# Rounding by ACT, preparation in gaps, and the last expert products between the first blocks of the closing layer

## The chip, the core and the metric

The kernel runs on one core of a Trainium2 chip. The core has a matrix engine (PE), a vector engine (DVE), an engine for functions of one operand (ACT), a general engine (POOL), and queues that issue DMA transfers (SP's and ACT's for plain ones, POOL's for gathers by index). Each engine takes its instructions in the order in which the program lists them and waits on semaphores for the others. The metric is the device time of one execution in microseconds (us); lower is better.

## The reference, cut to what matters

Three steps run in a row: attention with keys and values pooled by 8 (8 batches, 8 heads, 576 tokens), a mixture of experts on its 4608 rows of 512, and a last layer.

```python
# experts: every row goes to the two best of 8
h = np.maximum(x[mask] @ w1[e], 0.0)                  # 512 -> 1024
out[mask] += top2_w[mask, k, None] * (h @ w2[e])      # 1024 -> 512
# last layer
h = x @ w_in                                          # 512 -> 2048
g = h * np.cos(h)
return (g @ w_out).astype(np.float32)                 # 2048 -> 512
```

## The kernel before

Every product of two float32 matrices is made from float16 halves: a value is a high part plus a rest, and three matmuls (high by high, high by rest, rest by high) give one product.

**Experts.** Rows are scattered to slots of their expert in memory. An expert's slots come in three chunks (`CH`): 512, 512 and 192. A job is one expert and one chunk, and `JOBS` lists them. A job makes eight first products (`mm1`, 12 matmuls each, with a relu on ACT and a rest on DVE behind each) and, for every 128 slots, one last product (`mm2`, 24 matmuls of 512 columns); `mix` spreads the last products of a job between the first products of the next. In the chunks of 192 the last 64 slots of two experts share one product (`mm2_pair`). ACT scales a finished product and stores it in `yb`. The program is one list, `work`; `begin` gives each entry a nominal time from its matmul columns, and `at` hangs other steps behind the first entry at or after a nominal time. So the order is written out by hand on every queue.

**Preparation of a chunk for the last layer.** A chunk is four tiles of 128 rows, and there are nine. Its steps: `gather` (POOL fetches the two expert rows of each row by index), `comb1a` (ACT) and `comb1b` (DVE) add them with their gates and take maxima, `comb2a` and `comb2b` make a scale from the chunk's maximum (through a small transpose on PE), and for each of seven operands `sub` (DVE), `opa` (ACT, high part), `opb` (DVE, rest, and a transposing DMA on SP's queue) fill the tile `xt_tile(c, o)`. Chunk 0 is prepared by `prepare_first` during the experts, at nominal times; chunk c + 1 by `prepare` while chunk c runs.

**Last layer.** A chunk runs in four quarters (`q_`) of its 2048 hidden columns. A quarter makes seven products (`prod`, numbers 1, 2, 6, 7, 5, 3, 4; 12 matmuls of 256 columns each) from which sums give four blocks of h, a scheme with seven products in place of eight. Each block then goes through `act_a` (DVE adds and subtracts a large constant, which rounds, and subtracts the rounded from the block; ACT takes the Sin and the Square) and `act_b` (DVE multiplies, ACT and POOL split the result into halves). The product with w_out (`down`, 3 matmuls of 512 columns each, 16 for a quarter) is listed in `ds` and taken from it by `some(n)` between the products of the following quarter. Products 1, 6, 5 and 3 use one PSUM bank (`pb`), so that each of the last three waits until ACT has copied the one before (copies at L1282, L1294 and L1302). `step` takes the next entry of the preparation at fixed places. The halves of w_out are loaded by `load_wout` into the buffers that the last two experts' `w2` leave.

Of the kernel before, what the change touches and what calls it, by code (L numbers as in the profile page):

```python
# [22 lines left out]
CAP = 1216  # L23
# [11 lines left out]
def tile_attn_moe_ffn(ctx: ExitStack, tc: tile.TileContext, q, k, v, wgate, wnoise, noise,  # L35
# [745 lines left out]
    JOBS = [(e, c) for e in range(E) for c in ((0, 1, 2) if e % 2 == 0 else (2, 0, 1) if e < E - 1 else (0, 2, 1))]  # L781
# [35 lines left out]

    def mm2(j, t):
        e, c = JOBS[j]
# [4 lines left out]
        ps = psum("py", 2)  # L824
        i = 0
        for f in range(8):
            for a_, b_ in ((0, 0), (0, 1), (1, 0)):
                PE.matmul(ps[0:m], ht[:, a_, f, 128 * t:128 * t + m], w[:, b_, f, :], start=(i == 0), stop=(i == 23))  # L828
                i += 1
        yt = wp.tile([128, 512], F32, name="yt", bufs=2)  # L830
        A.activation(yt[0:m], ps[0:m], AF.Copy, scale=W["y", e][0:m])  # L831
        r0 = E * o + n * e + 128 * t
        A.dma_start(yb[r0:r0 + m, :], yt[0:m])

    def mm2_pair(e):
        ps = psum("py", 2)

        w = [W["w2", e + i].rearrange("p s (k f) -> p s k f", k=8) for i in range(2)]
        i = 0
        for f in range(8):  # L840
            for a_, b_ in ((0, 0), (0, 1), (1, 0)):
                for h in range(2):
                    PE.matmul(ps[64 * h:64 * h + 64], TAIL[e + h][:, a_, f, :], w[h][:, b_, f, :], start=(i == 0),  # L843
                              stop=(i == 23))
                i += 1
        yt = wp.tile([128, 512], F32, name="yt", bufs=2)
        for h in range(2):
            hs = slice(64 * h, 64 * h + 64)
            A.activation(yt[hs], ps[hs], AF.Copy, scale=W["y", e + h][hs])
        for h in range(2):  # L850
            r0 = E * 1024 + (CAP - 1024) * (e + h) + 128
            A.dma_start(yb[r0:r0 + 64, :], yt[64 * h:64 * h + 64])
# [259 lines left out]
    def prepare(c, room):  # L1112


        def many(*x):
            return lambda: [f(c, *a) for f, *a in x]

        return [many((gather, 0), (gather, 1)),
                many((gather, 2), (gather, 3), (comb1a, 0), (comb1a, 1)),
                many((comb1b, 0), (comb1b, 1), (comb1a, 2), (comb1a, 3)),  # L1120
                many((comb1b, 2), (comb1b, 3), (comb2a,)),
                many((comb2b,), (opa, 0), (opa, 1), (opa, 2, room)),
                many((opb, 0), (opb, 1), (opb, 2), (sub, 3)),
# [222 lines left out]
```

## Time and profile before

| | |
|---|---|
| median of three runs | 1885.58 us (1883.87 to 1886.46) |
| profiled execution | 1891.88 us, span of the program 1890.1 us |
| PE busy | 1745.7 us, 92% of the span |
| DVE busy | 1193.2 us, 63% |
| ACT busy | 838.9 us, 44% |
| POOL busy | 421.6 us, 22% |
| DMA, mean over the span | 129 GB/s |

Busy is the time in which an engine works on an instruction; matmuls are pipelined and their ends are modelled, so that two that follow each other overlap a little. A row of a timeline gives the start in the span, the length, the engine, the line of the kernel, the operation, what it writes and reads, how many like it are merged, and in brackets how long the engine stood idle before it and what ended that.

### The profile page before, as it was taken

What the parts mean: (1) busy time and instruction counts of PE and PEld (TensorE: products, weight loads), DVE (VectorE), ACT (ScalarE), POOL (GpSimd) and SP (SyncE); (2) the same over time, 40 slices, a digit from 0 to 9 for tenths busy, and PEclk for the clock granted to TensorE, in tenths of its full rate; (3) what the DMA queues carried; (4) which work ended last, traced back from release to release, by engine and by line L of the source; (5) the groups of instructions that cost most, each with busy time, mean ns of one, the idle gap of its engine ahead of it and who ended that gap; (6) DMA issues with size and microseconds to landing.
All of it is one profiled execution on the core that took longest, in us unless ns stands there. A gap on an engine that the chain in (4) does not pass through costs nothing.

```text
span 1890.1 us, 28449 instructions
## 1 busy us (share of the span) xinstructions
PE 1745.7 (92%) x11160; PEld 1028.8 (54%) x11160; DVE 1193.2 (63%) x2160; ACT 838.9 (44%) x1699; POOL 421.6 (22%) x457
## 2 busy tenths in 40 slices
PE   5977772899999999999999997999999999999999
PEld 3655551455444644464445544666666666666665
DVE  5784765453657375526774144877878777787864
ACT  4765651232333233323333233555555555555554
POOL 1225446000000000001110012244242334424222
PEclk8988876899999999999999998999999999999999
DMA  9968334457362846465644443124131212313100
GB/s 277 300 240 301 113 109 161 136 169 222 102 200 83 223 119 221 123 200 125 200 145 115 176 156 101 34 73 69 55 90 29 79 35 76 80 41 89 35 28 23
DMA packets 233209, 243.50 MB, mean 129 GB/s; under 512 B 154352, under 2 KB 167664, under 8 KB 232432
## 3 DMA queue, kind: packets, MB, share of 16 engines
q1 hardware_dynamic: 210544, 183.97, 33.9%
q0 software_dynamic: 11520, 37.76, 6.1%
q10 hardware_dynamic: 11008, 19.93, 3.0%
q8 instruction: 88, 1.44, 0.3%
q14 instruction: 49, 0.40, 0.1%
HBM read 127.06 MB, written 78.12 MB: 109 GB/s over the span
## 4 chain that ended last, share of the span: by engine, by line
PE 46%; DVE 19%; ACT 11%; issue 4%; DMA 2%; ACTq 0%; DVEq 0%; POOL 0%; POOLq 0%; SPq 0%
PE ph L803 20%; PE py L828 20%; DVE ty L1231 5%; ACT ty L1232 5%; DVE ty L1230 4%; ACT ty L1233 4%; PE ph L1253 3%; DVE ty L1241 2%; PE py L1223 2%; DMA yg<-yb,yidx 2%; DVE ht L1099 1%; DVE ht L1290 1%; DVE x2h L1099 1%; PE py L843 1%; DVE x L1047 1%
## 5 line engine op out<-in xcount | busy, mean ns | idle before, releaser
L803 PE MATMUL ph<-xt,w 128*128 128x512 f16 (+1 forms) x2304 | 410.4, 336 | 8.8 <-DMA xt<-xs 8.8
L1253 PE MATMUL ph<-w,ht 128*128 128x512 f16 x1728 | 413.5, 379 | 0.0
L828 PE MATMUL py<-w,ht 128*128 128x512 f16 x1728 | 384.4, 379 | 0.0
L803 PEld LDWEIGHTS <-w 128*128 128x128 f16 x2304 | 214.9, 98 | 195.2 <-issue 13.8
L1243 POOL TENSOR_TENSOR ht<-ty,ht 128x512 f16<-128x512 f32 x144 | 181.5, 1271 | 467.1 <-ACT ht L1242 390.5
L816 DVE SCALAR_TENSOR_TENSOR ht<-ph,ht 128x512 f16<-128x512 f32 (+2 forms) x192 | 110.0, 574 | 266.2 <-ACT ht L815 266.1
L828 PEld LDWEIGHTS <-ht 128*128 128x128 f16 x1728 | 168.7, 98 | 198.8 <-DVE ht L816 0.5
L1253 PEld LDWEIGHTS <-ht 128*128 128x128 f16 x1728 | 169.3, 98 | 152.1 <-issue 0.8
L1223 PEld LDWEIGHTS <-st 128*128 128x128 f16 x1872 | 184.0, 98 | 90.5 <-issue 42.7
L1232 ACT ACTIVATE ty<-ty,k 128x512 f32<-128x512 f32 x144 | 104.0, 722 | 261.9 <-DVE ty L1231 243.6
L815 ACT ACTIVATE ht<-ph 128x512 f16<-128x512 f32 (+2 forms) x192 | 96.3, 502 | 180.5 <-PE ph L803 154.5
L1223 PE MATMUL py<-xt,st 128*128 128x256 f16 x1040 | 142.4, 276 | 21.8 <-ACT ht L1302 10.8
L831 ACT ACTIVATE yt<-py,ysc 128x512 f32<-128x512 f32 x72 | 49.4, 686 | 228.2 <-PE py L828 223.4
L1241 DVE SCALAR_TENSOR_TENSOR ty<-ty,ht 128x512 f32<-128x512 f32 x108 | 74.8, 692 | 110.7 <-ACT ty L1233 108.9
L1223 PEld LDWEIGHTS <-w 128*128 128x128 f16 x1152 | 113.2, 98 | 36.9 <-issue 1.0
L1223 PE MATMUL py<-w,st 128*128 128x256 f16 x832 | 111.7, 272 | 9.4 <-ACT ht L1294 6.7
L1032 POOL DMA_INDIRECT yg<-yb,yidx x72 | 73.4, 1020 | 162.9 <-DMA yb<-yt 93.5
L1231 DVE TENSOR_TENSOR ty<-ht,ty 128x512 f32<-128x512 f32 x108 | 104.9, 972 | 3.7
L894 POOL TENSOR_TENSOR tm<-yg 128x512 f32<-128x512 f32 x32 | 33.8, 1055 | 302.6 <-DVE x L904 150.5
L1242 ACT ACTIVATE ht<-ty 128x512 f16<-128x512 f32 x144 | 90.1, 626 | 24.6 <-DVE ty L1241 24.4
L450 PE MATMUL xp<-vbd,et 128*64 128x144 f32 (+3 forms) x864 | 80.5, 326 | 17.7 <-DVE g_u L492 17.7
L1230 DVE TENSOR_SCALAR ty<-ht,k 128x512 f32<-128x512 f32 x108 | 91.1, 843 | 7.7
(249 smaller groups left out, 2141.6 us busy)
## 6 DMA issues: line engine op xcount, KB each, us to landing
yb<-yt ACTq DMA_DIRECT2D x72, 256.0 KB
st<-in_moe_w_dram SPq DMA_DIRECT2D x8, 2048.0 KB
yg<-in_moe_w_in_dram SPq DMA_DIRECT2D x32, 512.0 KB
yg<-in_moe_w_out_dram SPq DMA_DIRECT2D x32, 512.0 KB
yb<-zt SPq DMA_DIRECT2D x18, 768.0 KB
st<-in_moe_w_dram SPq DMA_DIRECT2D x8, 1536.0 KB
w<-in_k_dram SPq DMA_DIRECT2D x16, 512.0 KB
w<-in_v_dram SPq DMA_DIRECT2D x16, 512.0 KB
```

The costliest lines, as they stand in the source:

```text
L803: PE.matmul(ps[:, 0:n], w[:, a_, k_, 128 * f:128 * f + 128], xt[:, 4 * b_ + k_, 0:n], start=(i == 0), stop=(i == 11))
L815: A.activation(t[:, 0], p, AF.Relu)
L816: V.scalar_tensor_tensor(t[:, 1], p, 0.0, t[:, 0], op0=OP.max, op1=OP.subtract)
L828: PE.matmul(ps[0:m], ht[:, a_, f, 128 * t:128 * t + m], w[:, b_, f, :], start=(i == 0), stop=(i == 23))
L1223: PE.matmul(o, FW["in"][4 * a_ + 2 * sa + k_][:, f:f + 128], x[:, :, sb, k_, :], start=(start and h == 0 and k_ == 0 and j == 0), stop=(k_ ...
L1230: V.tensor_scalar(y, h, k4[:, 0:1], k4[:, 0:1], op0=OP.add, op1=OP.subtract)
L1231: V.tensor_sub(y, h, y)
L1232: A.activation(y, y, AF.Sin, scale=k4[:, 1:2])
L1241: V.scalar_tensor_tensor(y, y, CC, h, op0=OP.subtract, op1=OP.mult)
L1242: A.activation(g[:, 2 * b, :], y, AF.Copy)
L1243: PL.tensor_sub(g[:, 2 * b + 1, :], y, g[:, 2 * b, :])
L1253: PE.matmul(ps, g[:, 2 * b + a_, 256 * h + 128 * tt:256 * h + 128 * tt + 128], FW["out"][b_][:, k_, :], start=(q_ == 0 and b < 2 and h == ...
```

## The change

- `JOBS`: the last expert's chunks go in the order 0, 1, 2; before, 0, 2, 1.
- `mm2` and `mm2_pair` can be made in parts. The last `mm2` (of the last expert's chunk of 192) and the last `mm2_pair` leave `work` and become the first eight entries of `ds`, four parts each, in the PSUM banks `ph`. They are taken between the products of chunk 0's first quarter, and `load_wout` moves in there.
- `prepare_first`: nominal distances of 1.3 instead of 1.8, and the steps from 15 on (`own_first`) go into chunk 0's first quarter.
- `act_a` and `act_b` become five steps placed one by one. `act_r`: ACT adds the constant. `act_t`: one DVE operation subtracts the constant and the block. `act_s`: Sin and Square. `act_b`: DVE's product. `act_g`: the split by ACT and POOL. The copy at what was L1294 stands ahead of block 0's Sin and Square where it stood behind them.
- `prepare` returns steps under names of places in a quarter (A1, V1, V2, A2, V3, G1, G2) instead of one list; the gathers for a chunk come half a chunk earlier, from the third chunk on.

```diff
-    JOBS = [(e, c) for e in range(E) for c in ((0, 1, 2) if e % 2 == 0 else (2, 0, 1) if e < E - 1 else (0, 2, 1))]
+    JOBS = [(e, c) for e in range(E) for c in ((0, 1, 2) if e % 2 == 0 or e == E - 1 else (2, 0, 1))]
...
+    def parts(k_, fs, ps, done):
+        st = []
+        n = len(fs) // k_
+        def part(i):
+            def f():
+                if i == 0:
+                    st.append(ps())
+                for m in fs[n * i:n * i + n]:
+                    m(st[0])
+                if i == k_ - 1:
+                    done(st[0])
+            return f
+        return [part(i) for i in range(k_)]
...
+        if c == 1:
+            put_(0, "G1", (gather, 0), (gather, 1))
+            put_(0, "G2", (gather, 2), (gather, 3))
+            put_(1, "A1", (comb1a, 0), (comb1a, 1))
+            put_(1, "V2", (comb1b, 0), (comb1b, 1))
+            put_(1, "A2", (comb1a, 2), (comb1a, 3))
+            put_(1, "V3", (comb1b, 2), (comb1b, 3), (comb2a,))
+            put_(2, "A1", (comb2b,))
+        else:
+            put_(0, "A1", (comb1a, 0), (comb1a, 1), (comb1a, 2))
+            put_(0, "V2", (comb1b, 0))
+            put_(0, "A2", (comb1a, 3))
+            put_(0, "V3", (comb1b, 1))
+            put_(1, "V1", (comb1b, 2))
+            put_(1, "V2", (comb1b, 3), (comb2a,))
+            put_(1, "V3", (comb2b,))
+        put_(2, "A1", (opa, 0), (opa, 1), (opa, 2, room))
+        put_(2, "V1", (opb, 0))
+        put_(2, "V2", (opb, 1), (sub, 3))
+        put_(2, "A2", (opa, 3))
+        put_(2, "V3", (opb, 2), (sub, 4), (sub, 5))
+        put_(3, "A1", (opa, 4), (opa, 5, room))
+        put_(3, "V1", (opb, 3), (sub, 6))
+        put_(3, "V2", (opb, 4), (opb, 5))
+        put_(3, "A2", (opa, 6))
+        put_(3, "V3", (opb, 6))
+        if c + 1 < NCF:
+            for q_ in (2, 3):
+                st[q_, "G1"] = [lambda i=i: gather(c + 1, i) for i in (2 * q_ - 4, 2 * q_ - 3)]
+        return st
...
-    for j in range(NJ + 1):
+    for j in range(NJ):
...
-    sched[work.index((mm2_pair, E - 2))].append(load_wout[0])
...
+    own_first = []
...
-            at(begin[o] + 12 + 1.8 * (t - 3), f)
+            (own_first.append if t >= 15 else lambda f: at(begin[o] + 12 + 1.3 * (t - 3), f))(f)
...
-    def act_a(c, q_, b, h):
-
-        k4 = CB["k4", c]
+    def act_r(c, q_, b, h):
+
         y = wp.tile([128, 512], F32, name="ty", bufs=4)
-        V.tensor_scalar(y, h, k4[:, 0:1], k4[:, 0:1], op0=OP.add, op1=OP.subtract)
-        V.tensor_sub(y, h, y)
-        A.activation(y, y, AF.Sin, scale=k4[:, 1:2])
+        A.activation(y, h, AF.Identity, bias=CB["k4", c][:, 0:1])
+        UB[b] = (c, q_, h, y)
+
+    def act_t(b):
+
+        c, _, h, y = UB[b]
+        V.scalar_tensor_tensor(y, y, CB["k4", c][:, 0:1], h, op0=OP.subtract, op1=OP.subtract)
+
+    def act_s(b):
+
+        c, _, _, y = UB[b]
+        A.activation(y, y, AF.Sin, scale=CB["k4", c][:, 1:2])
         A.activation(y, y, AF.Square, scale=math.sqrt(2.0 * CC))
...
-    load_wout[1]()
-    ds, st = [], []
+
+    bank = lambda: psum("ph", 4)
+    ds = mm2_pair_parts(E - 2, 4, bank) + mm2_parts(NJ - 1, 0, 4, bank)
...
             prod(c, q_, 1, pb, True)
             A.activation(cw[:, 0], pb, AF.Copy)
-            act_b(2)
-            if q_ == 0 and c and st:
-                step()
-            if q_ == 0 and c + 1 < NCF or q_:
-                step()
+            if 2 in UB:
+                act_b(2)
+                act_g(2)
+            if c == 0 and q_ == 0:
+                for f in own_first:
+                    f()
+                some(1)
+            at_("A1")
+            at_("V1")
             some(2)
             prod(c, q_, 2, pa, True)
             V.tensor_add(cw[:, 0], pa, cw[:, 0])
-            act_a(c, q_, 0, cw[:, 0])
+            act_r(c, q_, 0, cw[:, 0])
+            act_t(0)
             some(2)
             prod(c, q_, 6, pb, False)
             A.activation(cw[:, 1], pb, AF.Copy)
+            act_s(0)
+            at_("V2")
+            if c == 0 and q_ == 0:
+                load_wout[0]()
             some(2)
             prod(c, q_, 7, pc, True)
+            if c == 0 and q_ == 0:
+                some(1)
+                load_wout[1]()
             act_b(0)
-            if len(st) > 1 or q_ < 3:
-                step()
+            act_g(0)
+            at_("G1")
+            at_("A2")
+            at_("V3")
             some(1)
             prod(c, q_, 5, pb, False)
             A.activation(cw[:, 2], pb, AF.Copy)
             V.tensor_add(cw[:, 2], pc, cw[:, 2])
-            act_a(c, q_, 3, cw[:, 2])
+            act_r(c, q_, 3, cw[:, 2])
+            act_t(3)
             some(2)
             prod(c, q_, 3, pb, False)
-            act_a(c, q_, 1, pb)
+            act_r(c, q_, 1, pb)
+            act_t(1)
+            act_s(3)
+            act_s(1)
             act_b(3)
+            act_g(3)
+            at_("G2")
             some(1)
             prod(c, q_, 4, pc, False)
             V.tensor_add(cw[:, 1], pc, cw[:, 1])
+            act_r(c, q_, 2, cw[:, 1])
             act_b(1)
-            act_a(c, q_, 2, cw[:, 1])
+            act_t(2)
+            act_g(1)
             some(16)
+            act_s(2)
```

## Rows read from the trace of the kernel before

**Rows 1.** The profile's page: busy time of each engine, and from its list of groups the Sin (line, engine, operation, tiles, shapes, count | busy us, mean ns | idle us before it and what ended it).

```profile
PE 1745.7 (92%) x11160; PEld 1028.8 (54%) x11160; DVE 1193.2 (63%) x2160; ACT 838.9 (44%) x1699; POOL 421.6 (22%) x457
...
L1232 ACT ACTIVATE ty<-ty,k 128x512 f32<-128x512 f32 x144 | 104.0, 722 | 261.9 <-DVE ty L1231 243.6
```

**Rows 2.** The table of stretches in the last layer: the stretch, its length, busy us (and instructions) of PE, PE's weight loads, DVE, ACT and POOL, granted clock of PE, share of the DMA engines, GB/s.

```profile
1306.16:1327.66 21.50, 19.85 (x133) 12.88 (x132) 13.52 (x17) 11.90 (x20) 13.81 (x14) 1.00 0.41 111
...
1817.26:1836.79 19.53, 19.53 (x134) 12.91 (x133) 12.20 (x16) 11.01 (x18) 4.76 (x5) 1.00 0.11 42
1190.00:1870.00 680.00, 661.43 (x4436) 433.64 (x4434) 508.96 (x730) 381.92 (x617) 227.68 (x190) 1.00 0.22 57
```

**Rows 3.** The waits of PE from 1190 us to the end: who waited for whom, us in total, times, longest.

```profile
PE py L1223 <- ACT ht L1294: 13.2, 23, 1.1
PE py L1223 <- ACT ht L1302: 4.8, 7, 1.3
```

**Rows 4.** The timeline of the quarter that begins at 1306.16, around PE's wait: the sum on DVE, the Sin, the copy, the product that waits.

```profile
1313.16 0.68 DVE L1290 TENSOR_TENSOR ht<-pt,ht 128x512 f32<-128x512 f32 x1
...
1315.32 0.72 ACT L1232 ACTIVATE ty<-ty,k 128x512 f32<-128x512 f32 x1 [3.25 <-DVE ty L1231]
...
1316.61 0.58 ACT L1294 ACTIVATE ht<-py 128x512 f32<-128x512 f32 x1
...
1317.24 1.47 PE L1223 MATMUL py<-xt,st 128*128 128x256 f16 x12 [1.14 <-ACT ht L1294]
```

**Rows 5.** Single lines of the kernel over the span: line, engine, operation, count, shortest/median/longest in ns, first and last start, shapes.

```profile
L1230 DVE TENSOR_SCALAR ty<-ht,k x108: 545/548/1408, 1142.9 to 1873.9; 128x512 f32<-128x512 f32 x108
L1230 DVE TENSOR_SCALAR ty<-py,k x36: 799/805/811, 1158.9 to 1870.3; 128x512 f32<-128x512 f32 x36
...
L1231 DVE TENSOR_TENSOR ty<-ht,ty x108: 691/693/1529, 1143.5 to 1875.4; 128x512 f32<-128x512 f32 x108
...
L1241 DVE SCALAR_TENSOR_TENSOR ty<-ty,ht x108: 682/692/694, 1145.6 to 1878.4; 128x512 f32<-128x512 f32 x108
...
L1243 POOL TENSOR_TENSOR ht<-ty,ht x144: 1152/1161/1612, 1153.5 to 1879.8; 128x512 f16<-128x512 f32 x144
```

**Rows 6.** The timeline of PE from the last experts into the last layer, and its last stretch. L803 is `mm1`, L828 `mm2`, L843 `mm2_pair`, L1223 `prod`, L1253 `down`.

```profile
1064.25 2.14 PE L803 MATMUL ph<-xt,w 128*128 128x192 f16 x24
...
1080.55 5.34 PE L828 MATMUL py<-w,ht 128*128 128x512 f16 x24
...
1086.82 0.40 PE L843 MATMUL py<-w,ty 128*64 128x512 f16 x1
...
1092.12 2.76 PE L803 MATMUL ph<-xt,w 128*128 128x512 f16 x12
1094.72 5.34 PE L828 MATMUL py<-w,ht 128*128 128x512 f16 x24
1099.90 10.52 PE L803 MATMUL ph<-xt,w 128*128 128x512 f16 x48
...
1118.57 20.88 PE L828 MATMUL py<-w,ht 128*128 128x512 f16 x96
1139.29 1.47 PE L1223 MATMUL py<-xt,w 128*128 128x256 f16 x12
...
1156.14 2.71 PE L1223 MATMUL py<-xt,st 128*128 128x256 f16 x12 [8.54 <-ACT ht L1302]
...
1162.18 1.47 PE L1223 MATMUL py<-xt,w 128*128 128x256 f16 x12 [0.78 <-DVE ht L1311]
...
1174.76 2.61 PE L1223 MATMUL py<-xt,st 128*128 128x256 f16 x12 [2.62 <-ACT ht L1294]
...
1186.18 1.47 PE L1223 MATMUL py<-xt,w 128*128 128x256 f16 x12
...
1871.96 14.41 PE L1253 MATMUL ph<-w,ht 128*128 128x512 f16 x66
```

**Rows 7.** The timeline of DVE, ACT and POOL in the same stretch: a gather (L1032), two combinations (L1047), a rest and the wait for its landing (L1099, L1095), the combination that waits for a gather (L1041) and the copy behind it (L1302).

```profile
1089.59 1.02 POOL L1032 DMA_INDIRECT yg<-yb,yidx  x1 [93.50 <-DMA yb<-yt]
...
1105.31 0.74 DVE L1047 SCALAR_TENSOR_TENSOR x<-yg,gates,x 128x512 f32<-128x512 f32 x1
...
1106.69 0.74 DVE L1047 SCALAR_TENSOR_TENSOR x<-yg,gates,x 128x512 f32<-128x512 f32 x1
...
1114.83 0.74 DVE L1099 SCALAR_TENSOR_TENSOR x2h<-x,xt4s,x2h 128x512 f16<-128x512 f32 x1
...
1118.47 0.72 ACT L1095 ACTIVATE x2h<-x,xt4s 128x512 f16<-128x512 f32 x1 [1.69 <-DMA xt<-x2h]
...
1152.17 0.72 ACT L1041 ACTIVATE x<-yg,gates 128x512 f32<-128x512 f32 x1 [5.18 <-DMA yg<-yb,yidx]
...
1155.52 0.58 ACT L1302 ACTIVATE ht<-py 128x512 f32<-128x512 f32 x1
```

**Rows 8.** The issue of w_out's second half on SP's queue (timeline), and two rows of the table of stretches (columns as in rows 2).

```profile
1139.49 0.32 SPq L1177 DMA_DIRECT2D w<-woutd  x1
...
1140.00:1144.00 4.00, 4.00 (x40) 3.59 (x38) 1.75 (x3) 0.78 (x2) 0.00 (x0) 1.00 0.94 324
...
1172.00:1176.00 4.00, 1.38 (x8) 0.92 (x7) 2.42 (x5) 2.47 (x4) 0.32 (x1) 0.86 0.00 0
```

**Rows 9.** The groups of ACT over the span: all loads of a table of functions.

```profile
L60 ACT ACT_TABLE_LOAD x1 | 1.3, 1283 | 0.7 <-PEq L1331 0.7
L730 ACT ACT_TABLE_LOAD x1 | 1.3, 1283 | 0.0
```

More of the change, by code (lines that the diff above doesn't have):

```diff
@@ L816, in mm1, with mm2_parts @@
             V.scalar_tensor_tensor(t[:, 1], p, 0.0, t[:, 0], op0=OP.max, op1=OP.subtract)
+    def parts(k_, fs, ps, done):
[11 more added lines that the diff above has]
+        return [part(i) for i in range(k_)]
     def mm2(j, t):
+        for f in mm2_parts(j, t, 1, lambda: psum("py", 2)):
+            f()
+    def mm2_parts(j, t, k_, bank):
         e, c = JOBS[j]
@@ L823, in mm2, with done, mm2_pair_parts @@
         ht = HT[j]
-        ps = psum("py", 2)
-        i = 0
+        fs = []
         for f in range(8):
             for a_, b_ in ((0, 0), (0, 1), (1, 0)):
[L828 to L833, printed above, removed]
+                fs.append(lambda ps, i=len(fs), f=f, a_=a_, b_=b_: PE.matmul(
+                    ps[0:m], ht[:, a_, f, 128 * t:128 * t + m], w[:, b_, f, :], start=(i == 0), stop=(i == 23)))
+        def done(ps):
+            yt = wp.tile([128, 512], F32, name="yt", bufs=2)
+            A.activation(yt[0:m], ps[0:m], AF.Copy, scale=W["y", e][0:m])
+            r0 = E * o + n * e + 128 * t
+            A.dma_start(yb[r0:r0 + m, :], yt[0:m])
+        return parts(k_, fs, bank, done)
     def mm2_pair(e):
-        ps = psum("py", 2)
+        for f in mm2_pair_parts(e, 1, lambda: psum("py", 2)):
+            f()
+    def mm2_pair_parts(e, k_, bank):
         w = [W["w2", e + i].rearrange("p s (k f) -> p s k f", k=8) for i in range(2)]
-        i = 0
+        fs = []
         for f in range(8):
@@ L842, in mm2_pair, with done @@
                 for h in range(2):
[L843 to L852, printed above, removed]
+                    fs.append(lambda ps, i=len(fs) // 2, f=f, a_=a_, b_=b_, h=h: PE.matmul(
+                        ps[64 * h:64 * h + 64], TAIL[e + h][:, a_, f, :], w[h][:, b_, f, :], start=(i == 0), stop=(i == 23)))
+        def done(ps):
+            yt = wp.tile([128, 512], F32, name="yt", bufs=2)
+            for h in range(2):
+                hs = slice(64 * h, 64 * h + 64)
+                A.activation(yt[hs], ps[hs], AF.Copy, scale=W["y", e + h][hs])
+            for h in range(2):
+                r0 = E * 1024 + (CAP - 1024) * (e + h) + 128
+                A.dma_start(yb[r0:r0 + 64, :], yt[64 * h:64 * h + 64])
+        return parts(k_, fs, bank, done)
     def y_rows():
@@ L1112, in prepare, with put_ @@
     def prepare(c, room):
[L1115 to L1123, printed above, removed]
-                many((sub, 4), (sub, 5), (opa, 3), (opa, 4), (opa, 5, room)),
-                many((opb, 3), (opb, 4), (opb, 5), (sub, 6)),
-                many((opa, 6), (opb, 6))]
+        if c >= NCF:
+            return {}
+        st = {}
+        def put_(q_, p_, *x):
+            st.setdefault((q_, p_), []).extend((lambda f=f, a=a: f(c, *a)) for f, *a in x)
+        if c == 1:
[28 more added lines that the diff above has]
+        return st
     load_x(0)
@@ L1268, in some, with at_ @@
         del ds[:n]
-    def step():
-        if st:
-            st.pop(0)()
     for c in range(NCF):
+        plan = prepare(c + 1, lambda: g[:, 14:16, :])
         for q_ in range(4):
-            if q_ == 0 and c + 1 < NCF:
-                st += prepare(c + 1, lambda: g[:, 14:16, :])
+            def at_(p_):
+                for f in plan.pop((q_, p_), []):
+                    f()
             g = GQ[c, q_] = wp.tile([128, 16, 512], F16, name="ht", bufs=2)
```

10 lines of the change are left out of this document (5 added, 5 removed).

## The prediction, made before the change was run

> **What bounds the kernel now.** I read the page first: the matrix engine (PE) is busy for 1745.7 of 1890.1 us [rows 1], so only its idle time can be won. The table of stretches then shows where the change can reach. From 1190 to 1870 us, the last layer, PE is busy for 661.43 of 680 us at full granted clock [rows 2]. A quarter of a chunk in which nothing waits (1817.26 to 1836.79) takes 19.53 us, all of it busy; the quarter at 1306.16 takes 21.50 us [rows 2]. The view of waits gives the cause: PE waits 13.2 us for the ACT copy at L1294 and 4.8 us for the one at L1302 [rows 3].
>
> The timeline of such a quarter shows why the copy is late [rows 4]. ACT takes its instructions in order. The copy of product 6 (L1294) stands behind the Sin and the Square of block 0, the Sin waits 3.25 us for DVE's two rounding operations, and DVE reaches the sum at L1290 late because of preparation work. PE then stands 1.14 us. Over the span the Sin stands 243.6 us idle behind DVE [rows 1].
>
> The second place is the passage from the experts to the last layer, 1080 to 1186 us. The PE timeline shows chunk 0's first quarter lasting from 1139.29 to 1162.18 and the second to 1186.18, with waits of 8.54 and 2.62 us [rows 6]. ACT's copy L1302 came late because the combination of the next chunk's rows stood ahead of it in the queue, 5.18 us waiting for a gather [rows 7]; that gather waits for the last expert's second chunk, which is the last thing that PE makes before the layer.
>
> **The rounding.** Each block loses one DVE instruction (548 ns from SBUF, 805 from PSUM) and has one of 693 ns (L1231) replaced by another two-input one; I price that by L1241, 692 [rows 5]. ACT gets one more per block, priced like the Sin with its per-partition operand, 722 ns [rows 1]. The bounds are 0.58 (the copy L1294, [rows 4]) and 0.72; both change nothing, since ACT is busy 11.90 of 21.50 us in a slow quarter [rows 2] and four more instructions make it 14.8 of 19.5.
>
> What decides is the order. After the change ACT does: add for block 0, copy of product 6, then Sin and Square. In the quarter shown, the sum starts at 1313.16 [rows 4]; with 0.69 for it and 0.72 for the add, ACT is free at 1314.6, the copy is done at 1315.2, and PE would come for it at 1316.1. It is 0.9 early instead of 1.14 late. What is late next? Product 3 needs the copy of product 5 with one pair of `down`s (1.30) as cover; copy and handoff take 0.8, so 0.5 is left. The first product of the next quarter needs the sum at L1311, which now stands behind the add, Sin and Square and the product of other blocks: 0.2 + 0.72 + 0.72 + 0.63 + 0.69 + 0.69 = 3.7 from the end of product 3, covered by a `down`, product 4 and six more `down`s, 5.8. Both covers hold.
>
> Sum: from 1186.18 to 1871.96 [rows 6] are 685.8 us for 34 quarters, less six `down`s left over (18 of the 66 matmuls of 14.41 us, 3.9). At 19.53 each that is 660.1 us. Of the 25.7 lost the two waits make 18.0 [rows 3], and their pipeline ends and other small delays the rest. I take back 23 and leave 0.08 a quarter.
>
> A rule speaks against this edit. The Trainium skill (ScalarE: Activation LUTs, section Rules for kernel authors) says that adds belong on VectorE, not ScalarE. By the instruction alone it would be right: 722 against 548 ns, 144 times, 25 us more engine time, and the sum would lose that if ACT were the bound. The trace doesn't bear it out here, since ACT stands 243.6 us waiting for DVE.
>
> **The passage.** The last expert's slots go in the order first, second, third chunk; the third's last product and the paired one leave the stretch before the layer and fill the first quarter. Lengths from [rows 6]: 12 matmuls of 512 columns 2.6 us, 12 of 192 columns 1.0, a last product of 24 5.2, the pair 5.3. The last `mm2` of the first chunk starts at 1080.55 now; seven first products of 2.6 instead of 1.0 stand before it, so 1091.8 then. From there the work alone is 5.2 + 2.6 + 8 x 1.0 + 4 x 5.2 = 36.6, the first quarter 19.53 - 10.5 (no `down`s yet) + 5.3 + 5.2 = 19.5, the second 19.53: it would end at 1167.4, 18.8 before today's 1186.18. I expect these stalls on it:
> - The PE transpose of the chunk's maximum is queued after the fifth first product of the last job, about 23.0 us after that `mm2`'s start. Its input comes after the rounding of the fourth product on DVE (22.9), two combinations at the pitch of 1.38 [rows 7], and 0.7 for maximum, copy and handoff: 26.4. So 3.4 us. Today's order, with 1.8 for 1.3 between the steps and longer products beside them, hides it.
> - Four operands of the layer's products are made inside the first quarter, on ACT, DVE and SP's queue. One goes from DVE to landed in 2.9 us (1115.57 to 1118.47, [rows 7]). Product 6 needs the sixth; by this chain it is there 11 us into the quarter, PE at 9.1: 1.8 us.
> - The copy of product 5 stands on ACT behind the eviction of the last expert's product (0.7) and the split of block 0 (0.6); they start 0.2 after that product, and product 5 covers 1.3 of this. With the copy's own 0.6 PE loses 0.9.
> - The quarter ends without `down`s, so of the 3.7 us above only 1.3 is covered: 2.4.
> - The second half of the layer's output weights (2048 KB) can be asked for only when the last expert part is done, 17.5 into the quarter. At 324 GB/s [rows 8] it takes 6.5 us, plus 3.2 for four gather transfers of 256 KB sharing the engines: landed at 24.4 to 27.6, and the first `down` comes at 25.9. I take 1.5, with 0 and 4 as bounds. SP's queue holds only later operands behind it, POOL's only the third chunk's gathers.
> - The clock. After 2.62 us of idle PE the granted clock was 0.86 over 1172 to 1176 [rows 8], between the levels of 2.4 and 1.2 GHz, and 12 matmuls took 2.61 instead of 1.47 us [rows 6]. For two stalls of that length I take 2.5, bounds 0 and 6.
>
> Together 12.5, so the passage gives 18.8 - 12.5 = 6.3, between 0 and 13. The gathers' own wait goes: the second chunk's rows are stored a whole job before. The new parts use the `ph` banks, free until the first `down`; the expert evictions move to ACT's idle time; the preparation's other steps are the same instructions at other places and cost nothing as long as DVE, lighter by some 2.4 us a quarter, keeps up.
>
> **The sum.** 23 + 6.3 = 29.3. The profiled execution took 1891.88 around its span of 1890.1 and would take 1862.6; it lies 6.3 above the median of the three runs, 1885.58, from which I take the same off: 1856.3, said as 1857. About 0.2% (4 us) is what this measurement can tell from no change.
>
> **Rivals.**
> - The wait moves (0.22). The new DVE operation of a block has two SBUF inputs like L1231, which went from 693 to 1529 ns [rows 5] where POOL's subtraction (1.16) ran. If sums or copies slip by that 0.8 behind a cover of 0.5, PE loses 0.2 to 0.5 us a quarter, 7 to 17 us: 1863 to 1874. Against it: DVE has less to do and the exposed block is the last of a quarter, with 3 us of cover.
> - The passage gives nothing (0.12): weights, gathers and clock take 6 to 12 more, the layer still gains its 23: 1862 to 1871.
> - Slower (0.09): ACT doesn't reach the copy of product 5 in time. With a Sin and Square of one block (1.35) ahead of it at that point, beyond the 0.5 of cover each us of lateness costs 34 us. It decides at 1.4 us of lateness, where the 29 is gone; at 2 us it is 1907. For it: 14.8 us of work in order in 19.5. Against it: nothing ahead of that copy waits for DVE's backlog any more.
> - The add needs another table of functions on ACT (0.02): two loads a block at 1283 ns [rows 9], 10.3 a quarter, ACT at 25 us a quarter: some 2060. Against it: the whole profile has two loads, though Relu, Copy, Square and Sin take turns. The Trainium skill (ScalarE: Activation LUTs, section Table sets: the hidden batching unit) has identity in every set as a cheap filler. By that no load comes; the trace agrees for Copy.
> - No change (0.03): DVE stays late from the preparation alone and the passage gives back the rest.
>
> **The numbers.** The forecast has 0.52, with a range of its own from 1848 to 1866 (25 and 12, or 18 and 2). The range reaches through the first two rivals and stops short of the others: 1847 to 1875, some 0.82. Faster 0.86, same 0.03, slower 0.11.
>
> **What would show it.** Right: in the stretch after the second quarter the waits of PE for the two copies sum to under 3 us, quarters of 19.5 to 19.7, DVE's share down and ACT's up by 12 to 15 points, no third table load. The first quarter starts near 1132 and the third near 1180, with stalls at the transpose, product 6 and the first `down`. Wrong: a quarter over 20 us in the steady part, a wait of PE on an ACT add, Sin or on L1311, or a start of the third quarter after 1186.

## The result and the profile after

The changed kernel takes 1854.05 us (median of six runs, 1850.7 to 1861.98), the kernel before, beside it, 1885.22 (1883.87 to 1892.08): a ratio of 0.9839 with a 95% interval of 0.9814 to 0.9865, so faster by 1.4 to 1.9%. The profiled execution took 1861.98 with a span of 1859.9, 29.9 below the 1891.88 of the one of before; the prediction's sum was 29.3.

The page of the changed kernel, busy time of each engine; before is [rows 1].

```profile
PE 1734.3 (93%) x11160; PEld 1025.2 (55%) x11160; DVE 1063.2 (57%) x2016; ACT 928.3 (50%) x1843; POOL 424.0 (23%) x457
```

DVE has lost 130 us and ACT gained 89.

The table of stretches of the changed kernel (columns as in [rows 2]): the whole steady part, the first quarter of chunk 2, and five short stretches of the passage, where the clock is of interest.

```profile
1200.00:1840.00 640.00, 639.93 (x4332) 423.51 (x4331) 374.98 (x574) 453.97 (x732) 221.18 (x184) 1.00 0.22 57
1297.80:1317.33 19.53, 19.53 (x134) 12.91 (x132) 10.01 (x15) 14.76 (x24) 4.46 (x4) 1.00 0.01 3
...
1116.00:1120.00 4.00, 1.85 (x9) 0.94 (x10) 3.60 (x15) 0.00 (x0) 0.00 (x0) 1.00 0.00 0
1120.00:1124.00 4.00, 4.00 (x24) 2.07 (x23) 0.05 (x1) 0.30 (x1) 0.00 (x0) 1.00 0.00 0
...
1152.00:1156.00 4.00, 2.21 (x21) 1.83 (x19) 2.51 (x5) 3.67 (x6) 2.99 (x4) 1.00 1.01 430
1156.00:1160.00 4.00, 3.20 (x16) 1.76 (x16) 2.30 (x3) 3.17 (x6) 3.47 (x4) 0.70 0.75 299
...
1160.00:1164.00 4.00, 4.00 (x25) 2.48 (x24) 1.39 (x2) 3.15 (x6) 3.38 (x4) 0.87 0.63 195
```

From 1200 to 1840 PE stands 0.07 us; the view of waits lists none on PE from 1190 to 1860, where before had 13.2 and 4.8 [rows 3]. The first quarter of chunk 2 takes 19.53 against 21.50 [rows 2]. In it, from the timeline of the changed kernel (L1355 the sum, L1360 the copy of product 6, L1294 the Sin):

```profile
1300.40 1.47 PE L1277 MATMUL pt<-xt,w 128*128 128x256 f16 x12
1301.97 0.69 DVE L1355 TENSOR_TENSOR ht<-pt,ht 128x512 f32<-128x512 f32 x1 [2.07 <-PE pt L1277]
...
1304.52 0.60 ACT L1360 ACTIVATE ht<-py 128x512 f32<-128x512 f32 x1 [1.04 <-PE py L1277]
1305.01 0.71 ACT L1294 ACTIVATE ty<-ty,k 128x512 f32<-128x512 f32 x1
```

DVE waits 2.07 us for PE and starts the sum 0.1 us after product 2, where before it started 2.8 us after it (mean of the first quarters of chunks 1 to 7, from the trace). ACT waits 1.04 for product 6 and copies it at once.

The timeline of PE in the passage of the changed kernel, the rows that wait and the ends of the stretch (L110 the transpose, L1277 `prod`, L1314 `down`); before is [rows 6].

```profile
1118.15 0.33 PE L110 MATMUL pt<-idf,mbc 128*128 128x128 f32 x1 [3.22 <-DVE mbc L104]
...
1131.65 1.47 PE L1277 MATMUL py<-xt,w 128*128 128x256 f16 x12
...
1142.43 1.48 PE L1277 MATMUL py<-xt,st 128*128 128x256 f16 x12 [1.07 <-DMA xt<-x2h]
...
1151.42 1.47 PE L1277 MATMUL py<-xt,st 128*128 128x256 f16 x12 [1.00 <-DMA yb<-yt]
...
1156.43 1.61 PE L1277 MATMUL py<-xt,w 128*128 128x256 f16 x12 [2.23 <-DVE ht L1392]
...
1158.83 2.29 PE L1314 MATMUL ph<-w,ht 128*128 128x512 f16 x5 [0.36 <-DMA w<-woutd]
...
1171.96 1.47 PE L1277 MATMUL py<-xt,st 128*128 128x256 f16 x12 [1.04 <-ACT ht L1377]
...
1175.20 0.38 PE L1277 MATMUL py<-xt,w 128*128 128x256 f16 x2 [1.11 <-DVE ht L1378]
...
1180.39 1.47 PE L1277 MATMUL py<-xt,w 128*128 128x256 f16 x12
...
1841.75 14.41 PE L1314 MATMUL ph<-w,ht 128*128 128x512 f16 x66
```

The third quarter starts at 1180.39 instead of 1186.18: the passage gave 5.8. From there to the last 66 matmuls it is 661.4 instead of 685.8 us: the steady part gave 24.4. Both are near the forecast. What each came from is another matter.

### The profile page after: what moved, and what is told of

It reads as the page before. It is cut to its first block, busy times and chain, and to the rows that moved or that the text cites. A ratio compares the mean times of both kernels' runs of the same rounds, so it can differ in the third digit from the quotient of the medians.

```text
span 1859.9 us, 28283 instructions
## 1 busy us (share of the span) xinstructions
PE 1734.3 (93%) x11160; PEld 1025.2 (55%) x11160; DVE 1063.2 (57%) x2016; ACT 928.3 (50%) x1843; POOL 424.0 (23%) x457
## 4 chain that ended last, share of the span: by engine, by line
PE 77%; ACT 2%; DVE 1%; DMA 1%; issue 0%; another core or an unknown queue 0%; ACTq 0%; SPq 0%
PE ph L803 21%; PE ph L1314 19%; PE py L847 19%; PE py L1277 14%; PE pt L1277 2%; PE py L869 1%; DMA xt<-x2h 1%; DMA xt<-xs 0%; DVE x L1076 0%; DVE ty L1289 0%; ACT ty L1283 0%; ACT ty L1294 0%; PE ph L847 0%; PE pt L110 0%; ACT x L1070 0%
## 5 line engine op out<-in xcount | busy, mean ns | idle before, releaser
L803 PE MATMUL ph<-xt,w 128*128 128x512 f16 (+1 forms) x2304 | 410.2, 336 | 9.0 <-DMA xt<-xs 9.0
L1314 PE MATMUL ph<-w,ht 128*128 128x512 f16 x1728 | 414.4, 380 | 0.4 <-DMA w<-woutd 0.4
L847 PE MATMUL py<-w,ht 128*128 128x512 f16 x1704 | 379.4, 379 | 0.0
L803 PEld LDWEIGHTS <-w 128*128 128x128 f16 x2304 | 214.8, 98 | 195.2 <-issue 13.1
L1314 PEld LDWEIGHTS <-ht 128*128 128x128 f16 x1728 | 169.5, 98 | 152.7 <-POOL ht L1304 0.8
L1277 PEld LDWEIGHTS <-st 128*128 128x128 f16 x1872 | 183.0, 98 | 55.5 <-issue 2.5
L852 ACT ACTIVATE yt<-py,ysc 128x512 f32<-128x512 f32 x71 | 48.7, 686 | 227.8 <-PE py L847 222.8
L1277 PE MATMUL py<-xt,st 128*128 128x256 f16 x1040 | 139.7, 273 | 3.1 <-DMA xt<-x2h 1.1
L1289 DVE SCALAR_TENSOR_TENSOR ty<-ty,k,ht 128x512 f32<-128x512 f32 x108 | 93.4, 865 | 82.2 <-ACT ty L1283 82.2
L1277 PEld LDWEIGHTS <-w 128*128 128x128 f16 x1152 | 112.8, 98 | 39.6 <-issue 4.8
L1294 ACT ACTIVATE ty<-ty,k 128x512 f32<-128x512 f32 x144 | 102.8, 714 | 21.0 <-DVE ty L1289 20.9
L1277 PE MATMUL py<-w,st 128*128 128x256 f16 x832 | 111.8, 273 | 0.0
L1283 ACT ACTIVATE ty<-ht,k 128x512 f32<-128x512 f32 x108 | 77.4, 717 | 68.1 <-DVE ht L1355 33.4
```

What stands on the lines that cost most here:

```text
L803: PE.matmul(ps[:, 0:n], w[:, a_, k_, 128 * f:128 * f + 128], xt[:, 4 * b_ + k_, 0:n], start=(i == 0), stop=(i == 11))
L847: fs.append(lambda ps, i=len(fs), f=f, a_=a_, b_=b_: PE.matmul(ps[0:m], ht[:, a_, f, 128 * t:128 * t + m], w[:, b_, f, :], start=(i == 0), ...
L1277: PE.matmul(o, FW["in"][4 * a_ + 2 * sa + k_][:, f:f + 128], x[:, :, sb, k_, :], start=(start and h == 0 and k_ == 0 and j == 0), stop=(k_ ...
L1283: A.activation(y, h, AF.Identity, bias=CB["k4", c][:, 0:1])
L1289: V.scalar_tensor_tensor(y, y, CB["k4", c][:, 0:1], h, op0=OP.subtract, op1=OP.subtract)
L1294: A.activation(y, y, AF.Sin, scale=CB["k4", c][:, 1:2])
```

## The experiments

Total times of one kernel scatter by some 10 us, and most of that lies ahead of the experts: their first product starts near 306 us in the traces of x5 to x8 and anywhere from 332.7 to 344.5 us in the others, while from there to the last expert's first product all take 687 to 688.5 us. The experiments were run in three groups, each with its own runs of before beside it: 1884.88 us for x1 to x4 (one execution each), 1853.82 for x5 to x8 (one each) and 1884.63 for the last four. So each run is read by two stretches of its own profile: the **passage**, from the last expert's first product to the third quarter of chunk 0, and the **steady** part, from there to the last 66 matmuls. All in us; the last columns are the time and that of before in the same group.

| kernel | passage | steady | time | before |
|---|---|---|---|---|
| before | 154.0 | 685.8 | | 1885.22 |
| after | 148.3 | 661.4 | 1854.05 | 1885.22 |
| x1: after, rounding on DVE again | 151.4 | 661.0 | 1859.28 | 1884.88 |
| x2: after, Sin and Square ahead of the copy again | 149.5 | 661.6 | 1856.49 | 1884.88 |
| x3: after, old list of preparation | 152.7 | 674.7 | 1878.97 | 1884.88 |
| x4: before, rounding on ACT alone | 154.3 | 736.5 | 1931.73 | 1884.88 |
| x5: before, copy ahead of Sin alone | 152.1 | 691.3 | 1856.90 | 1853.82 |
| x6: before, new places of preparation alone | 145.7 | 664.7 | 1823.97 | 1853.82 |
| x7: after, old order of the last expert | 144.5 | 661.1 | 1822.04 | 1853.82 |
| x8: after, later transpose | 144.8 | 661.4 | 1821.37 | 1853.82 |

**Rounding back on DVE (x1) and the old order on ACT (x2)**, each undone alone in the changed kernel.

In x1, in `act_r` and `act_t`:

```diff
-        A.activation(y, h, AF.Identity, bias=CB["k4", c][:, 0:1])
+        k4 = CB["k4", c]
+        V.tensor_scalar(y, h, k4[:, 0:1], k4[:, 0:1], op0=OP.add, op1=OP.subtract)
...
-        V.scalar_tensor_tensor(y, y, CB["k4", c][:, 0:1], h, op0=OP.subtract, op1=OP.subtract)
+        V.tensor_sub(y, h, y)
```

In x2, after product 6:

```diff
-            A.activation(cw[:, 1], pb, AF.Copy)
             act_s(0)
+            A.activation(cw[:, 1], pb, AF.Copy)
```

> The changed kernel with the rounding back on DVE (two operations, at the changed kernel's places); all else as changed. The steady stretch, from the start of chunk 0's third quarter to the 66 matmuls at the end, was 685.8 us before and 661.3 in the changed kernel. Theory 1 (order: what counts is that ACT copies product 6 before block 0's Sin and Square): 661 to 667, no wait of PE over 0.2 us a quarter. Theory 2 (load: what counts is DVE's work, 2.4 us a quarter less): back to 680 or more. Theory 3 (places of the preparation): 661 to 667.

> The changed kernel with block 0's Sin and Square ahead of the copy of product 6 again; rounding on ACT and the preparation as changed. Theory 1 (order): the wait for that copy is back, 0.3 us a quarter or more, steady stretch 672 to 686. Theory 2 (load) and theory 3 (places): 661 to 665. By the durations of the trace the copy would be done 0.7 to 1.5 us before PE wants it, which speaks against theory 1 in its strict form.

The table of stretches, x1:

```profile
1200.00:1820.00 620.00, 620.00 (x4201) 410.89 (x4199) 443.33 (x692) 363.70 (x587) 220.84 (x178) 1.00 0.22 59
```

and x2:

```profile
1200.00:1820.00 620.00, 619.94 (x4193) 409.71 (x4191) 367.88 (x563) 442.48 (x714) 213.38 (x179) 1.00 0.22 59
```

Neither loses anything in the steady part. In x1 DVE carries 75 us more than in x2 over the same 620 us and PE doesn't notice. In x2 the copy of product 6 starts up to 2.1 us after its product in chunks 1 to 7 and PE doesn't notice either: from the end of product 6 to the start of product 5 PE has 3.1 us of other work, and less the copy's 0.6 that covers about 2.5 us. Only in chunk 0's third quarter, where the copy starts 2.7 us late, does PE lose 0.2. x1's longer passage is one wait of 4.11 us for w_out and a stretch at a lower granted clock (0.50 from 1156 to 1160), in one execution. My theory, that rounding and order give the 23, had to go; what was left was the places of the preparation.

**The old preparation in the changed kernel (x3).**

```diff
-        plan = prepare(c + 1, lambda: g[:, 14:16, :])
...
-            at_("A1")
-            at_("V1")
+            if q_ == 0 and c and st:
+                step()
+            if q_ == 0 and c + 1 < NCF or q_:
+                step()
...
-            at_("G1")
-            at_("A2")
-            at_("V3")
+            if len(st) > 1 or q_ < 3:
+                step()
```

> The changed kernel with the old list of preparation steps, taken at the old two places of a quarter; rounding on ACT and the order of copy and Sin as changed. Theory 1 (order) and theory 2 (load): 661 to 667 for the steady stretch. Theory 3 (places): 672 or more, with the losses in the quarters that combine the rows (the first of a chunk, where ACT's copy of product 5 stands behind a combination).

The waits of PE in x3 from 1185 to 1860 (who waited for whom, us in total, times, longest; L1356 is the sum of product 7, L1355 the copy of product 5):

```profile
PE py L1252 <- DVE ht L1356: 7.1, 7, 1.0
PE py L1252 <- ACT ht L1355: 3.7, 6, 1.2
```

The steady part loses 13.3 of its 24.4, and the waits are back, at other instructions: the copy of product 6 is out of harm's way, the next two results aren't. Rounding, order and the separate split of `act_g` together are worth 11.1 where the preparation is in the old list.

**Rounding on ACT alone (x4), the copy ahead alone (x5)**, in the kernel before.

In x4, in `act_a`:

```diff
-        V.tensor_scalar(y, h, k4[:, 0:1], k4[:, 0:1], op0=OP.add, op1=OP.subtract)
-        V.tensor_sub(y, h, y)
+        A.activation(y, h, AF.Identity, bias=k4[:, 0:1])
+        V.scalar_tensor_tensor(y, y, k4[:, 0:1], h, op0=OP.subtract, op1=OP.subtract)
```

In x5, after product 6, with `act_a` for block 0 leaving out the Sin and the Square that `act_s` then makes:

```diff
             A.activation(cw[:, 1], pb, AF.Copy)
+            act_s(0)
```

> The kernel before with nothing but the rounding changed: ACT adds the constant, DVE subtracts it and the block in one operation; Sin and Square still stand ahead of the copy of product 6, preparation and passage as before. Theory 1 (order): the waits stay, steady stretch 680 to 688. Theory 2 (load): most of the gain is here, 661 to 668. Theory 3 (places): 678 to 688.

> The kernel before with one thing changed: the copy of product 6 stands ahead of block 0's Sin and Square on ACT. Rounding on DVE, preparation and passage as before. Theory 1 (order): the wait for that copy goes, steady stretch 664 to 672 (the 4.8 us of waits for the copy of product 5 may stay). Theory 2 (load): 680 or more. Theory 3 (places): 676 or more.

The waits of all engines in x4 from 1180 to 1900 (L1230 the add on ACT, L1231 DVE's subtraction, L1232 the Sin, L1294 the copy of product 6):

```profile
DVE ty L1231 <- ACT ty L1230: 169.0, 129, 2.0
ACT ty L1232 <- DVE ty L1231: 123.4, 127, 1.5
...
PE py L1223 <- ACT ht L1294: 43.2, 31, 2.1
```

the timeline of the first quarter of chunk 5 in x4:

```profile
1489.70 0.68 DVE L1290 TENSOR_TENSOR ht<-pt,ht 128x512 f32<-128x512 f32 x1
...
1490.48 0.72 ACT L1230 ACTIVATE ty<-ht,k 128x512 f32<-128x512 f32 x1 [1.86 <-DVE ht L1290]
...
1491.23 0.75 DVE L1231 SCALAR_TENSOR_TENSOR ty<-ty,k,ht 128x512 f32<-128x512 f32 x1 [0.85 <-ACT ty L1230]
...
1492.02 0.72 ACT L1232 ACTIVATE ty<-ty,k 128x512 f32<-128x512 f32 x1 [0.82 <-DVE ty L1231]
...
1493.31 0.58 ACT L1294 ACTIVATE ht<-py 128x512 f32<-128x512 f32 x1
...
1493.93 2.03 PE L1223 MATMUL py<-xt,st 128*128 128x256 f16 x12 [2.06 <-ACT ht L1294]
```

and, from its table of stretches, the second quarter of chunk 8:

```profile
1857.10:1876.63 19.53, 19.53 (x133) 12.91 (x132) 8.07 (x11) 12.90 (x22) 3.62 (x4) 1.00 0.14 52
```

Alone, the rounding edit makes the steady part 50.7 us longer, which none of the three theories foresaw. The block now goes from DVE to ACT, to DVE and to ACT again, both queues stand still at each handover, and the copy that PE waits for stands behind the chain: in a chunk's first quarter 2.06 us late instead of 1.14 [rows 4], in all 43.2 us of waits for it instead of 13.2 [rows 3]. The handovers do not cost that by themselves: beside chunk 8, the last, no other is prepared, and the quarter shown takes 19.53 with the new rounding as it did with the old [rows 2]. This is the Trainium skill's rule against adds on ScalarE (ScalarE: Activation LUTs, section Rules for kernel authors) that the prediction set aside: in x4 it holds, though for the queue's order, not for the instruction's own speed, which it speaks of. In the changed kernel the add costs nothing on either engine (661.4 on ACT, 661.0 on DVE in x1).

The waits of PE in x5 from 1146 to 1838 (L1308 is the copy of product 5):

```profile
PE py L1223 <- ACT ht L1308: 18.0, 7, 3.4
```

its timeline in the first quarter of chunk 2 (L1238 the Sin, L1041 a combination of the next chunk's rows):

```profile
1277.26 0.72 ACT L1238 ACTIVATE ty<-ty,k 128x512 f32<-128x512 f32 x1 [2.06 <-DVE ty L1231]
...
1282.34 0.72 ACT L1041 ACTIVATE x<-yg,gates 128x512 f32<-128x512 f32 x1 [1.69 <-DMA yg<-yb,yidx]
1282.96 0.58 ACT L1308 ACTIVATE ht<-py 128x512 f32<-128x512 f32 x1
```

and one of its stretches:

```profile
1200.00:1204.00 4.00, 3.81 (x18) 2.35 (x18) 2.87 (x5) 1.49 (x3) 2.84 (x3) 0.57 0.62 167
```

The 18.0 that before lost at two copies are 18.0 at one. The copy of product 5 stands behind what stood ahead of it before: block 0's Sin, Square and split and two combinations of the next chunk, one of which waits for its gather. It comes no earlier; PE only gets to it earlier. The steady part is 5.5 longer: 1.3 are waits for the sum of product 7, and PE is busy 4.2 longer (671.4 against 667.2), with the granted clock at 0.57 behind a wait of 2.40 in the stretch shown. The order that I called decisive moves the wait.

**The places of the preparation alone (x6).** The kernel before with the changed kernel's `prepare` and its seven places; nothing else of the change, neither rounding, order nor expert parts.

```diff
-            if q_ == 0 and c + 1 < NCF:
-                st += prepare(c + 1, lambda: g[:, 14:16, :])
+        plan = prepare(c + 1, lambda: g[:, 14:16, :])
...
+            at_("A1")
+            at_("V1")
...
             A.activation(cw[:, 1], pb, AF.Copy)
+            at_("V2")
...
+            at_("G1")
+            at_("A2")
+            at_("V3")
```

> The kernel before with the changed kernel's places of the preparation alone; rounding on DVE, Sin ahead of the copy, passage as before. Theory 1 (order) and theory 2 (load): the waits for the copy of product 6 stay in most quarters, steady stretch 676 or more. Theory 3 (places): 661 to 668. All of them: the 8.5 us wait in chunk 0's first quarter goes, since the next chunk's combination moves out of it.

x6's table of stretches:

```profile
1200.00:1600.00 400.00, 399.44 (x2695) 263.37 (x2694) 317.92 (x458) 236.14 (x383) 145.33 (x121) 1.00 0.26 65
```

its waits of PE from 1140 to 1800:

```profile
PE py L1248 <- ACT ht L1320: 1.3, 1, 1.3
```

and its timeline in the first quarter of chunk 2 (L1041 combinations on ACT, L1316 the sum, L1256 the rounding's second operation, L1257 the Sin, L1320 the copy of product 6):

```profile
1262.28 1.93 ACT L1041 ACTIVATE x<-yg,gates 128x512 f32<-128x512 f32 x3
...
1262.64 0.69 DVE L1316 TENSOR_TENSOR ht<-pt,ht 128x512 f32<-128x512 f32 x1 [0.93 <-PE pt L1248]
...
1264.80 0.72 ACT L1257 ACTIVATE ty<-ty,k 128x512 f32<-128x512 f32 x1 [0.59 <-DVE ty L1256]
...
1266.09 0.58 ACT L1320 ACTIVATE ht<-py 128x512 f32<-128x512 f32 x1
...
1268.24 1.47 PE L1248 MATMUL py<-xt,st 128*128 128x256 f16 x12
```

21.1 of the 24.4 us come from this edit by itself. The Sin's wait of 3.25 us [rows 4] is 0.59 and PE's of 1.14 is gone, although nothing is made faster. In the kernel before, the last rest of the preparation (L1099) stood on DVE right ahead of this sum and waited for ACT:

```profile
1312.10 1.14 DVE L1099 SCALAR_TENSOR_TENSOR x2h<-x,xt4s,x2h 128x512 f16<-128x512 f32 x1 [1.31 <-ACT x2h L1095]
```

In x6 that rest has its place in the quarter before, and in this quarter DVE's combinations stand behind the sum: DVE waits 0.93 us for PE and takes the sum as soon as it is there. The rest of the chain is the old one, the Sin still ahead of the copy, and the copy ends 1.6 us before the product that needs its bank (1266.09 + 0.58 against 1268.24). DVE is busy for 79% of the stretch, more than before's 75% [rows 2]; its load was not what counted. The passage falls to 145.7 too: the 8.54 us wait [rows 6] was an ACT combination that stood ahead of the copy waiting for a gather [rows 7], and it now has a place a quarter later.

Rounding and order add 3.3 to this: 1.4 in chunk 0's third quarter, where the 1.3 wait above lies, and 0.3 to 0.4 in the second quarter of six of the chunks 1 to 7.

**The experts' last products as before (x7) and the transpose later (x8)**, both in the changed kernel.

In x7, where the expert parts go unused, `JOBS`, `load_wout` and the preparation of chunk 0 (all of it ahead of the quarter, at 1.8) are as in the kernel before:

```diff
-    for j in range(NJ):
+    for j in range(NJ + 1):
...
-    ds = mm2_pair_parts(E - 2, 4, bank) + mm2_parts(NJ - 1, 0, 4, bank)
+    ds = []
```

In x8, in `prepare_first`:

```diff
-        st += [(8, lambda: comb2a(c)), (10, lambda: comb2b(c))]
+        st += [(8, lambda: comb2a(c)), (11, lambda: comb2b(c))]
```

> The changed kernel with the passage undone: the last expert's chunks in the old order, all its products ahead of the layer, weights loaded at the old places, chunk 0 prepared at the old distances; the layer as changed. In the changed kernel chunk 0's third quarter starts at 1180.4 us, before at 1186.2. Theory 1 (the products between the blocks give the passage's gain): the third quarter starts at 1184 or later. Theory 2 (the layer's own order took away the 8.5 us wait, and the products between the blocks give little or nothing, because the new order brings a 3.2 us wait at the transpose and others): 1176 to 1181, in spite of 10.5 us more in front of the layer.

> The changed kernel with one step of chunk 0's preparation one entry later: the PE transpose of the maximum behind the next last product instead of ahead of it. If the 3.2 us wait of PE there sets the start of the layer, that start moves from 1131.7 to 1128 to 1129 and the third quarter's from 1180.4 to 1177 to 1179. Rival: the operands of chunk 0 come as much later and PE waits for them inside the first quarter, so that the third quarter's start stays within 0.7 us of 1180.4.

With the old order of the experts the passage is 144.5, shorter by 3.7 than with the new one. The new one loses most of that in a single place, the 3.22 us at the transpose; x8 puts the step that holds it behind the next `mm2` and is at 144.8. So the products between the first blocks bring nothing here: without their stall they are level with the old order. That is one execution of each: the granted clock was 0.62 from 1116 to 1120 in x8 and 1.00 throughout these quarters in x7, so that a gain of up to 1.7 us isn't excluded.

The changed kernel, x6 and x7 once more, with a version that joins the old order to other places in chunk 0 (DVE's sum of product 4 ahead of block 3's product; in the first quarter the split of block 0 and the first gathers behind the copy of product 5; the other gathers behind block 1's split; part of the second quarter's combination behind block 3's split), five or six executions each:

> The changed kernel again, timed on the same chip as the three runs beside it. From the start of the last expert's first product to chunk 0's third quarter 148 to 149 us (before 154.0), steady stretch 661.4 (before 685.8): ratio to the kernel before 0.983 to 0.985.

> The kernel before with the places of the preparation alone, timed. If these carry the change, and the passage of the changed kernel costs more than it gives, this is as fast as the changed kernel: stretches of 145.7 and 664.7 by its first profile, ratio 0.983 to 0.986. If rounding and passage add what they seem to by the profile of the changed kernel (as the prediction has it), the changed kernel is faster by 10 us or more.

> The changed layer behind the old passage, timed. By the first profile 144.5 and 661.1 us for the two stretches: 3.5 to 4.5 us faster than the changed kernel, ratio 0.980 to 0.983. If the products between the first blocks give the passage's gain, it is 5 us slower than the changed kernel.

> The changed layer behind the old passage, with chunk 0's first two quarters put right by what their waits show: the sum of product 4 ahead of block 3's product on DVE, block 0's split behind the copy of product 5, the second pair of gathers behind block 1's split, half of the next chunk's combination behind block 3. The waits of 1.75, 2.23, 1.03, 1.79 and 1.11 us shrink to 2 to 4 in sum, so the first stretch falls from 144.5 to 139 to 142 and the time by 3 to 5 us against the old tail. Rival: the steps moved back delay the third quarter's operands, and the sum of the waits stays within 1 us.

| kernel | passage | steady | time | ratio to before (95%) |
|---|---|---|---|---|
| after | 151.0 | 661.3 | 1856.85 | 0.9848 (0.9822 to 0.9874) |
| places alone (x6) | 145.6 | 664.7 | 1850.91 | 0.9826 (0.9796 to 0.9856) |
| old order of the experts (x7) | 144.6 | 661.1 | 1851.05 | 0.9830 (0.9803 to 0.9856) |
| x7 with chunk 0 rearranged | 143.3 | 661.0 | 1850.97 | 0.9823 (0.9794 to 0.9852) |

The stretches repeat to 0.2 us, but for the passage of after, where I expected 148 to 149. The times can't separate the four: the intervals overlap, as differences of 1 to 8 us in 1850 make one expect. By the sum of the two stretches the four save 27.5, 29.5, 34.2 and 35.4 us against the kernel before: the places alone give about as much as the whole change. The rearranged chunk 0 misses the 139 to 142 that I expected. It saves 2.4 us in the first quarter (11.0 against 13.5) and gives half back in the second, by ACT's queue (L1377 the copy of product 5, L1305 a split that waits for DVE, L1070 a combination, both ahead of the copy):

```profile
1158.73 0.63 ACT L1305 ACTIVATE ht<-ty 128x512 f16<-128x512 f32 x1 [3.15 <-DVE ty L1300]
1159.27 1.32 ACT L1070 ACTIVATE x<-yg,gates 128x512 f32<-128x512 f32 x2
1160.49 0.57 ACT L1377 ACTIVATE ht<-py 128x512 f32<-128x512 f32 x1
...
1161.12 1.47 PE L1279 MATMUL py<-xt,st 128*128 128x256 f16 x12 [3.79 <-ACT ht L1377]
```

## Why the prediction was right in its number and wrong in its cause

**The steady part: 23 forecast, 24.4 measured, by the wrong step.** The number was right because I took nearly all of the 25.7 lost as the gain: any edit that ends both waits gives about that, so it says little for the edit that I credited. The bound, the two waits, the quarter of 19.53 and the waits' sum were right, and so were the signs to look for (no wait, quarters of 19.53 to 19.9, ACT 14.76 of 19.53, two table loads). The step that failed is "What decides is the order". Order alone costs 5.5 (x5), rounding alone 50.7 (x4), both together, with the separate split, give 11.1 on the old list (x3), and undone one at a time in the changed kernel they are worth nothing (x1, x2). The step beside it that failed is that the preparation's other steps "cost nothing as long as DVE, lighter by some 2.4 us a quarter, keeps up": they were costed by their busy time, which is the same, and their places are worth 21.1 alone (x6). The prediction had named the cause itself ("DVE reaches the sum at L1290 late because of preparation work") and put its remedy elsewhere. The rows had it, too: the quarter of 1817.26, in the chunk beside which no other is prepared, takes 19.53 with the old rounding and the old order [rows 2]. I read it as the ideal time and didn't ask what it lacked.

**Why the gains don't add.** The copy of product 6 has some 2.5 us of cover. Before, it started 2.7 to 3.6 us after its product (mean over chunks 1 to 7, by quarter, worked out from the three traces), in x6 0.9 to 2.4, in the changed kernel 0.04. Either remedy, order or places, brings this copy under its cover; what it is early beyond that is worth nothing.

**ACT late at the copy of product 5, the rival on the other side**, was real as a mechanism: it is x5 and a part of x3. In the changed kernel the places keep DVE, and so what ACT waits for, ahead of it, and one combination instead of two stands there, its rows fetched half a chunk earlier. The cover of 0.5 that I gave that copy held: it starts 0.04 us after its product, and PE doesn't wait. The load of 14.8 was right.

**The passage: 6.3 forecast, 5.8 measured.** The starts of the first and third quarter, 1131.65 and 1180.39, are where I put them (1132, 1180). Term by term: transpose 3.4, measured 3.22; product 6 1.8, measured 1.07; copy of product 5 0.9, measured 1.00; end of the quarter 2.4, measured 2.23; weights 1.5, measured 0.36; the clock 2.5, of which the granted 0.70 and 0.87 of two stretches of 4 us make at most 1.7. (The row of the 1.00 names a DMA, but the copy of product 5 on ACT ended 0.05 us before that product started.) The weights were there 27.2 us into the quarter, at the late end of my 24.4 to 27.6; PE came for them at 26.8 instead of 25.9. Other executions show how loose that term is: the wait was 4.11 in x1 and 1.00 in the changed kernel's second trace. Not foreseen: 1.04 and 1.11 in the second quarter, behind the next chunk's combination. So the 5.8 is partly luck: product 6, weights and clock were put 2.7 too high, and the two waits not foreseen make 2.2. But here too the credit was misplaced: the wait of 8.54 that I took away by the new order of the expert's chunks goes by the gathers' and combinations' places alone (x6, 145.7), and the new order costs 3.7 of it (x7).

**The rivals.** The moved wait showed at one place. The subtraction that I feared beside POOL took 2.08 in chunk 0's second quarter, with POOL's rests beside it, against 0.75 elsewhere; it lies ahead of the 1.04 there. In the steady part it found cover. No table load came: ACT has two in the changed kernel and in x4, as before [rows 9]. The Trainium skill (ScalarE: Activation LUTs, section Table sets: the hidden batching unit) has identity, the function of the new add, in every set; the trace agrees. "No change", at 0.03, named what x4 and x5 then showed: DVE stays late from the preparation alone.

**Left open.** Why the rounding with the old list costs 50.7 in the old order and is part of a gain with the new one (x3) was followed to the waits of x4 and to the preparation beside them, not taken apart further. x3 holds rounding, order and the separate split together. x6 fetches rows earlier and spreads the other steps at once; what each gives was not tried.

## What to carry to other kernels

When an in-order engine is late, list what stands ahead of the late instruction in its queue and when each of these could go at the latest; moving side work behind a hand-over can give what no faster instruction gives, and moving the instruction to another engine can add two hand-overs in place of one, which cost where side work stands between them. Look for a stretch of the old trace that has no loss and ask what work it lacks: that is an experiment already made. A sum that comes out right says nothing of its terms: undo each part alone, and do each alone, before crediting it.

## What the runs showed of the hardware

The granted clock didn't follow the length of a wait alone. 3.22 us at the transpose left it at 1.00 in the changed kernel (1116 to 1124 above); in its profiled execution of the last group a wait of 3.15 at the same instruction was followed by half clock, the 1.2 GHz level. From that one's table of stretches:

```profile
1112.00:1116.00 4.00, 4.00 (x11) 1.47 (x10) 0.52 (x4) 0.00 (x0) 0.00 (x0) 0.50 0.00 0
1116.00:1120.00 4.00, 4.00 (x30) 2.47 (x29) 0.00 (x0) 0.74 (x2) 0.00 (x0) 0.97 0.00 0
```

In the first, the clock fell only between 1156 and 1160 (0.70 above), behind shorter waits (1.00 and 2.23). In x5 it was 0.62 from 1694 to 1698, behind a wait of 2.04, and 1.00 from 1283 to 1287, behind one of 3.17. One kernel so started its closing layer 99.5 and 102.3 us after the last expert's first product; its first two quarters took 48.7 us both times, and the passage 148.3 and 151.0.

A DVE operation with two inputs from SBUF was held while POOL subtracted. From the timeline of x7 (L1290 the subtraction of the rounding, L1305 two of POOL's rests):

```profile
1123.66 2.28 POOL L1305 TENSOR_TENSOR ht<-ty,ht 128x512 f16<-128x512 f32 x2
1123.73 2.77 DVE L1290 SCALAR_TENSOR_TENSOR ty<-ty,k,ht 128x512 f32<-128x512 f32 x1 [1.93 <-ACT ty L1284]
```

It ends 0.56 us behind POOL's second, and takes 2.77 instead of 0.75. The Trainium skill says that, of two such operations, the one that starts first has the shared port for its whole length and the other blocks (SBUF — State Buffer, section SBUF: two separate sides); the trace agrees, and shows DVE's blocked through two of POOL's in a row.
